# A folded Fourier transform: matmuls of 32 rows in four tiles in place of 64 rows in two

## The chip, the cores and the metric

The kernel runs on one core of a Trainium2 chip. The core has a matrix engine (PE; its weight loads are shown apart as PEld), three engines for elementwise work (VectorE, shown as DVE; ScalarE, ACT; GpSimd, POOL) and SyncE (SP), which here only issues DMAs. Matmuls write to PSUM, eight banks of 2 KB per partition; all other on-chip data lie in SBUF. [...] The metric is the device time of one execution in microseconds; lower is better. All data are float32.

## The reference

```python
batch, seq, dim = (8, 3008, 256)
X = np.fft.fft(x, axis=1)
X = np.fft.fft(X, axis=2)
x = X.real.reshape(8 * 3008, 256)
gate = 1.0 / (1.0 + np.exp(-(x @ w_gate)))      # w_gate, w_val: 256 x 1536
val = x @ w_val
out = gate * val @ w_out                        # w_out: 1536 x 256
```

A real Fourier transform over 3008 positions and over 256 features, and behind it a gated feed-forward layer.

## The kernel before

**Transform.** M = 1504 is half the sequence. By the symmetries of cosine and sine, positions and features are folded: rows that share a table entry up to sign are added first (`fold_ops`, line 398, mostly on POOL), and a matmul then contracts fewer rows against a table of cosines and sines. Batch 0 contracts 128 partitions x NQ = 6 row groups. Batches 1 to 7 are folded once more: `mirror_x` (line 151) writes a copy of x to DRAM, `XR`, in which partitions 0 to 63 hold even rows, 64 to 127 odd ones, and row groups 3 to 5 the mirrored rows; `load_x` (line 144) brings it back as tile `x4`. `turn` (line 449) adds to the odd block a multiple of the even one with VectorE (L454).

The matmuls of one batch are `whole` (line 531), called for the odd and the even block (`blk` 1, 0) and for cosine and sine (`what` 0, 1). `both` (line 493) issues 12 matmuls of about 63 rows x 189 columns each time: the even rows into bank `ev`, the odd rows into bank `od`, on the two halves of the array. The bank pair changes with `what`. `then` (line 507) copies with ACT (L512, L518), adds with VectorE (L514) and `places` (line 522) writes the outputs to rows of `pk` and `qk` (L524, L528), which hold the transform of one batch with 1505 frequencies.

**Feed-forward.** The work behind it goes in *fronts*. A front i is one block of 128 of the 1536 hidden features for one chunk of up to 252 frequencies; 12 fronts make a chunk and 6 chunks, 72 fronts, a batch. In the code and in the prediction a front of a batch is counted from the batch's first front, `s0`. Each front does, in this order of recording:

- `front_a` (line 631): PE, four records `pf<-pk` into one of three `pf` banks, after `seed` (line 622, L629) on ACT has written a starting value there.
- `gate_a` (line 651) of the front before: ACT sigmoid L658, DVE subtraction L659.
- `part` (line 640): ACT copies `pf` to `ae` (L644). Then the seed of the next front.
- `gate_b` (line 666) of the front before: DVE product L671, ACT sigmoid L672, DVE product L675, then sums on POOL (L681).
- `back` (line 714): PE, ten records `po<-h` or `po<-sf` of the output matmul, five fronts late. After the last group of a chunk the five `po` banks are copied out by ACT and DVE (L748).
- `front_b` (line 646): PE, four records `pf<-qk` into the same bank, after `part`.
- two or three jobs from the list `later`: the sums of `finish` on DVE (L765), transposes (L773), and stores.
- the side jobs that `at(i, ...)` has put on this front.

So the order on each engine is written out by hand: an engine takes its instructions in the order in which they are recorded, and waits on semaphores inside it. The side jobs fix where the next batch's fold, its turn, its transform and its loads stand. The transform of batch b + 1 is put at front g0 = s0 + 40 of batch b (at 64 for b = 0), after `front_b`. The matmul of the transform uses the same `po` banks as `back`, which is why it stands where a chunk has just been finished. Tables for batches 1 to 7 are loaded and built during batch 0 (`table_again`, line 193, and `table_odd`, line 206).

## Time and profile before

| | |
|---|---|
| median of 3 runs | 1923.05 us (1923.03 to 1923.23) |
| span of the profiled execution | 1921.4 us |
| DVE, ACT, POOL busy | 74%, 70%, 79% |
| PE records of the transform, batches 1 to 7 | 672 `ev` and `od` matmul records in all |
| DVE additions L514 in it | 56, 17.1 us |
| DVE L454 (`turn`) | 42, 29.1 us |
| DVE sums L765 | 920, 430.5 us, 500 ns each |
| POOL sums L681 | 2392, 1334 us |
| DMA | 97.02 MB, mean 50 GB/s |
| PE clock granted | 1.00 |

A row of a timeline reads: start, duration, engine, line, operation, output<-inputs, shape and number; in brackets idle time before it and what ended it. The trace shows two records for each matmul. Most matmuls are recorded on line 134, in the helper `mm`, so they are told apart by the names of their tiles. The duration of a record contains latency: back to back, a record takes the distance between two starts. The profiled span lacks what lies around it: the median of the runs is 1.65 us longer.

### The profile page before, as it was taken

Reading aid. Unit: us, or ns where it says so; the run is one execution under the profiler, and the core shown is the slowest. Engines: PE = TensorE matmul, PEld = TensorE weight load, DVE = VectorE, ACT = ScalarE, POOL = GpSimd, SP = SyncE. Lnnn points to the kernel's source line nnn. Section 1 sums busy time; section 2 is a strip of 40 time slices with the busy share of each in tenths; the row PEclk is TensorE's granted clock in tenths of the full one; section 3 lists DMA queues with packets and bytes.
Section 4 is the critical chain, followed back from the end, with each engine's and each line's share of the span. In section 5 each row is a group of like instructions: output and inputs, shape, how many; then the busy total and the mean of one; then the engine's idle time right before and its main releaser. Section 6 shows DMA issues by size and latency. Waiting matters only on the chain.

```text
span 1921.4 us, 34211 instructions
## 1 busy us (share of the span) xinstructions
PE 1910.5 (99%) x11164; PEld 1776.2 (92%) x11164; DVE 1429.4 (74%) x3225; ACT 1344.2 (70%) x3148; POOL 1524.8 (79%) x2733
## 2 busy tenths in 40 slices
PE   8999999999999999999999999999999999999999
PEld 5789999999999999999999999999999999999998
DVE  7677877787777777778677777777777687777775
ACT  4876767767777677776777767777677767777775
POOL 2489969978898788987888878888788977877770
PEclk9999999999999999999999999999999999999999
DMA  8353222120131211202111121121200100011011
GB/s 313 110 98 78 66 80 60 48 80 15 22 78 23 80 20 41 61 14 82 26 47 48 20 84 19 47 52 23 80 15 15 27 15 15 14 21 21 15 16 31
DMA packets 173633, 97.02 MB, mean 50 GB/s; under 512 B 134429, under 2 KB 164360, under 8 KB 171664
## 3 DMA queue, kind: packets, MB, share of 16 engines
q1 hardware_dynamic: 172878, 94.32, 20.2%
q8 instruction: 90, 1.47, 0.3%
q14 instruction: 87, 0.71, 0.1%
q10 hardware_dynamic: 546, 0.51, 0.1%
q0 software_dynamic: 32, 0.00, 0.0%
HBM read 70.08 MB, written 46.71 MB: 61 GB/s over the span
## 4 chain that ended last, share of the span: by engine, by line
PE 98%; DMA 1%; DVE 1%; ACT 0%; issue 0%; SPq 0%; ACTq 0%
PE pf L134 51%; PE po L134 43%; PE ev L134 3%; DMA x<-in_xf_dram 1%; PE od L134 1%; PE ps L134 1%; DMA raw<-in_moe_w_val_dram 0%; PE pe L134 0%; DVE z L659 0%; DVE wf L307 0%; ACT wl L389 0%; DVE x L418 0%; DVE x L469 0%; DVE x L405 0%; ACT ae L644 0%
## 5 line engine op out<-in xcount | busy, mean ns | idle before, releaser
L681 POOL TENSOR_TENSOR sf<-h 128x168 f32<-128x168 f32 (+1 forms) x920 | 511.0, 575 | 215.5 <-DVE h L675 215.2
L681 POOL TENSOR_TENSOR sf<-h,sf 128x168 f32<-128x168 f32 (+1 forms) x1104 | 616.4, 579 | 56.5 <-DVE h L675 56.2
L134 PE MATMUL pf<-pk,G 128*128 128x252 f32 (+1 forms) x2304 | 582.7, 376 | 0.0
L134 PE MATMUL pf<-qk,G 128*128 128x252 f32 (+1 forms) x2304 | 582.1, 375 | 0.2 <-ACT ae L644 0.2
L675 DVE TENSOR_TENSOR h<-pf,z 128x252 f32<-128x252 f32 (+1 forms) x576 | 241.7, 420 | 418.5 <-ACT pf L672 418.5
L629 ACT ACTIVATE pf<-ek,ge 128x252 f32<-128x252 f32 (+1 forms) x1142 | 538.1, 471 | 20.4 <-DMA ge<-G 1.0
L134 PE MATMUL po<-sf,wf 128*128 128x168 f32 (+1 forms) x2944 | 508.2, 305 | 0.0
L644 ACT ACTIVATE ae<-pf 128x504 f32<-128x504 f32 (+1 forms) x576 | 339.7, 590 | 233.8 <-PE pf L134 232.5
L134 PEld LDWEIGHTS pf<-pk,G 128*128 128x128 f32 x2304 | 436.7, 190 | 52.6 <-issue 2.3
L134 PEld LDWEIGHTS po<-sf,wf 128*128 128x128 f32 x2944 | 453.4, 190 | 8.0
L134 PE MATMUL po<-h,wf 128*128 128x168 f32 (+2 forms) x2584 | 459.6, 306 | 0.0
L134 PEld LDWEIGHTS pf<-qk,G 128*128 128x128 f32 x2304 | 411.0, 190 | 30.4 <-issue 1.8
L765 DVE TENSOR_TENSOR c<-c 128x168 f32<-128x168 f32 (+1 forms) x920 | 430.5, 500 | 4.8
L134 PEld LDWEIGHTS po<-h,wf 128*128 128x128 f32 x2584 | 411.4, 190 | 17.0 <-issue 0.9
L659 DVE TENSOR_TENSOR z<-ae,pf 128x504 f32<-128x504 f32 (+1 forms) x576 | 383.7, 666 | 33.2 <-ACT h L658 31.7
L658 ACT ACTIVATE h<-pf 128x252 f32<-128x252 f32 (+1 forms) x576 | 218.2, 379 | 163.5 <-PE pf L134 159.4
L672 ACT ACTIVATE pf<-z 128x252 f32<-128x252 f32 (+1 forms) x576 | 214.2, 372 | 79.5 <-DVE h L671 76.6
L671 DVE TENSOR_TENSOR h<-h,pf 128x252 f32<-128x252 f32 (+1 forms) x576 | 233.0, 404 | 0.0
L681 POOL TENSOR_TENSOR sf<-sf 128x168 f32<-128x168 f32 (+1 forms) x184 | 106.0, 576 | 14.4
L681 POOL TENSOR_TENSOR sf<-sf,h 128x168 f32<-128x168 f32 (+1 forms) x184 | 100.7, 547 | 0.0
L748 ACT COPY c<-po 128x504 f32<-128x504 f32 (+1 forms) x138 | 78.5, 569 | 0.0
L773 DVE STREAM_TRANSPOSE os<-c 128x256 f32<-128x256 f32 x188 | 72.4, 422 | 0.4 <-issue 0.3
(139 smaller groups left out, 899.8 us busy)
## 6 DMA issues: line engine op xcount, KB each, us to landing
x<-xr SPq DMA_DIRECT2D x14, 1536.0 KB
out_dram<-os SPq DMA_DIRECT2D x368, 56.0 KB
xr<-in_xf_dram SPq DMA_DIRECT2D x14, 768.0 KB
xr<-in_xf_dram SPq DMA_DIRECT2D x35, 256.0 KB
ek<-ed SPq DMA_DIRECT2D x40, 126.0 KB
out_dram<-os SPq DMA_DIRECT2D x284, 7.0 KB
x<-in_xf_dram SPq DMA_DIRECT2D x3, 1024.0 KB
st<-in_stab_dram SPq DMA_DIRECT2D x3, 753.0 KB
```

Source lines behind the costliest of these rows:

```text
L134: nc.tensor.matmul(o, l, r, start=start, stop=stop, skip_group_check=True)
L629: nc.scalar.activation(PF[i][:, g], EK[i // NFT], AF.Copy, scale=ge[:, g, f : f + 1])
L644: nc.scalar.activation(AP[i], PF[i], AF.Copy, scale=2.0)
L658: nc.scalar.activation(H[p][:, fh, 0:n], PF[i][:, 0], AF.Sigmoid)
L659: nc.vector.tensor_tensor(z[:, :, ::-1], AP.pop(i), PF[i], op=ALU.subtract)
L671: nc.vector.tensor_tensor(h[:, fh, 0:n], h[:, fh, 0:n], pf[:, 1], op=ALU.mult)
L672: nc.scalar.activation(pf[:, 0], z[:, 0], AF.Sigmoid)
L675: nc.vector.tensor_tensor(h[:, fh, n:], pf[:, 0], z[:, 1], op=ALU.mult)
L681: nc.gpsimd.tensor_tensor(block(p, dst), block(p, a), block(p, b), op=(ALU.subtract, ALU.add)[op])
L748: (nc.vector.tensor_copy if t == 1 or t == 3 else nc.scalar.copy)(C[0][:, 3 * t * R : 3 * (t + 1) * R], PO[t][:, 0 : 3 * R])
L765: nc.vector.tensor_tensor(t[:, dst * R : (dst + 1) * R], *v, op=(ALU.subtract, ALU.add)[op])
L773: nc.vector.transpose(os_[0][:, s, 0:nb, h, :], t[:, c0 : c0 + nb * TB])
```

## The change

Batches 1 to 7 are folded once more, row s with row 376 - s. A batch's rows then lie in four groups of 32 partitions (even and odd rows, each plain and mirrored at 376), and each matmul contracts 31 or 32 rows against about 95 table columns, one group into one PSUM bank. What the fold would have to add across partitions before the matmuls is added in part before (`more`) and in part after them.

- `mirror_x` issues 23 DMAs per batch and not 9, of 32 rows each and not 64.
- `table_rows` writes mirrored table rows to DRAM in batch 0; `table_again` loads the tables in 16 DMAs and not 4, and `table_ops` builds them on DVE, POOL and ACT in fronts 45 to 52.
- `swap`: 16 DMAs per batch exchange halves of `x4` between partition groups. `more`: 15 `scalar_tensor_tensor` instructions per batch on DVE add a multiple of what was exchanged: nine of 256 columns, six of 128. `turn` stays and comes earlier.
- `whole` now issues all 96 matmuls of a batch at one place, in four stages of 24. The four tiles take turns from instruction to instruction. After each stage two banks are copied to SBUF by ACT and two by DVE.
- `whole_ops` adds the parts later, from SBUF: 28 instructions on DVE per batch, at fronts s0 + 48 to s0 + 51 and s0 + 60 to s0 + 63 (for batch 1 at 66 to 69 and 72 to 75, half of them on POOL).
- The transform stands after `front_a` of front g0 + 1, and the `back` of front g0 is recorded ahead of `gate_b`.

```diff
+            def swap(blk):
+                hs, here, there = (((1, 3), slice(0, HD), slice(HD, D)), ((0, 2), slice(HD, D), slice(0, HD)))[blk]
+                for g, par, lo in TILES:
+                    o = lo + (TB, -TB)[g]
+                    for h in hs:
+                        nc.sync.dma_start(out=x4[lo : lo + TB, h, :, there], in_=x4[o : o + TB, h, :, here])
+
+            def more(v, blk, c, q):
+                here, there = ((slice(0, HD), slice(HD, D)), (slice(HD, D), slice(0, HD)))[blk]
+                here, there = (v[..., ds] for ds in (here, there))
+                nc.vector.scalar_tensor_tensor(out=here, in0=there, scalar=c[:, q : q + 1], in1=here,
+                                               op0=ALU.mult, op1=ALU.add)
...
-    def whole(b, blk, what):
-        _, then, both = seq_group(b, blk, what, (2, 3) if what else (0, 1))
-        both()
-        return then()
+    def whole(b):
+        ps = [bank("sum", t + 1) for t in range(4)]
+        n = 4 * NQ4
+        for blk in (1, 0):
+            for what in range(2):
+                for part in range(2):
+                    for q in range(N3):
+                        for t, (g, par, lo) in enumerate(TILES):
+                            rows = slice(lo, lo + TB - ((par, q) in ((0, 2), (1, 1), (1, 2))))
...
+                            c0 = (2 * what + 1 - part) * NQ4
+                            mm(ps[t][:, c0 : c0 + tab.shape[-1]], W[b, blk][what][rows, w], tab,
+                               what == part == q == 0, q == N3 - 1)
+                for t, (g, *_) in enumerate(TILES):
+                    cs = slice(2 * what * NQ4, 2 * (what + 1) * NQ4 - (not blk and (g + what) % 2))
+                    (nc.scalar.copy, nc.vector.tensor_copy)[t // 2](TAB["sums"][:, blk, t, cs], ps[t][:, cs])
...
+            t0, swaps, last = (47, (54, 57), 59) if b == 0 else (s0 + 24, (s0 + 29, s0 + 30), s0 + 35)
             for i, f in enumerate(TURN.pop(b + 1)):
-                at(58 + i if b == 0 else slots[-1] - 1 + i * 4 // 6, f)
+                at(t0 + i if b == 0 else t0 + i * 4 // 6, f)
+            swaps_, more = MORE.pop(b + 1)
+            for i, f in zip(swaps, swaps_):
+                at(i, f)
+            for i, f in enumerate(more):
+                at(last + i * 5 // 6, f)
...
-        for blk in (1, 0):
-            at(g0, *[lambda b=b, blk=blk, what=what: whole(b + 1, blk, what)() for what in range(2)])
+        mid[g0 + 1] = lambda b=b: whole(b + 1)
+
+        def ends_(b=b, g0=g0):
+            low, high = whole_ops(b + 1, (nc.vector, nc.gpsimd) if b == 0 else (nc.vector, nc.vector))
+            n0 = g0 + (2 if b == 0 else 8)
+            for i, f in enumerate(low):
+                at(n0 + i, f)
+            n0 = g0 + (8 if b == 0 else 20)
+            for i, f in enumerate(high):
+                at(n0 + i, f)
...
+        if i + 1 in mid:
+            back((i - 5) // 3, (i - 5) % 3)
         if i:
             gate_b(i - 1, *join.pop(i, []))
         for f in pre.pop(i, []) + out_use.pop(i, []):
             f()
-        if i >= 5:
+        mid.get(i, lambda: None)()
+        if i >= 5 and i + 1 not in mid:
             back((i - 5) // 3, (i - 5) % 3)
```

## The prediction

> **What bounds the kernel now.** I read the first part of the page, then the waits, then the timeline of single engines around one transform and around one place where PE does stall. Part 1 and the chain of waits put the end on PE:

> ```profile
> PE 1910.5 (99%) x11164; PEld 1776.2 (92%) x11164; DVE 1429.4 (74%) x3225; ACT 1344.2 (70%) x3148; POOL 1524.8 (79%) x2733
> ```

> So every microsecond that PE stops issuing is added to the end, and every one that a matmul group loses is gained. The profiled span is 1921.4 us; the runs' median is 1923.05, so 1.65 us lie outside the span, and I add them at the end.

> The timeline of PE, batch 1:

> ```profile
> 256.78 0.42 PE L134 MATMUL ev<-st,x 63*128 63x189 f32 x1
> 256.79 0.42 PE L134 MATMUL od<-st,x 63*128 63x189 f32 x1
> 257.04 0.32 PE L134 MATMUL ev<-st,x 63*128 63x189 f32 x1
> 257.05 0.32 PE L134 MATMUL od<-st,x 63*128 63x189 f32 x1
> ...
> 265.05 1.10 PE L134 MATMUL pf<-pk,G 128*128 128x246 f32 x4
> ```

> A matmul leaves two records. The two members of a pair start 0.01 us apart, pairs follow each other every 0.16 us (257.04, 257.20, ...): 48 pairs, 8.27 us from 256.78 to 265.05. That is what the change can shorten, seven times 8.27 = 57.9 us.

> DVE works in a fixed round per front i: subtraction L659, product L671, wait for ACT's sigmoid, product L675. Where DVE is late the round has no slack left. From the timelines of DVE and then ACT, at fronts 40 to 45 of batch 0:

> ```profile
> 196.61 0.88 DVE L528 TENSOR_TENSOR er<-a 7x376 f32<-7x376 f32 x1
> 197.42 0.66 DVE L659 TENSOR_TENSOR z<-ae,pf 128x504 f32<-128x504 f32 x1
> 198.01 0.40 DVE L671 TENSOR_TENSOR h<-h,pf 128x252 f32<-128x252 f32 x1
> 198.86 0.42 DVE L675 TENSOR_TENSOR h<-pf,z 128x252 f32<-128x252 f32 x1 [0.45 <-ACT pf L672]
> 199.20 0.57 DVE L765 TENSOR_TENSOR c<-c 128x168 f32<-128x168 f32 x2
> ```
> ```profile
> 198.44 0.39 ACT L672 ACTIVATE pf<-z 128x252 f32<-128x252 f32 x1 [1.39 <-DVE h L671]
> 198.76 0.36 ACT L658 ACTIVATE h<-pf 128x252 f32<-128x252 f32 x1
> 199.02 0.58 ACT L644 ACTIVATE ae<-pf 128x504 f32<-128x504 f32 x1
> ```

> The reader is to see two numbers. The round takes 199.20 - 197.42 = 1.78 us at its shortest. And ACT's copy L644 of two fronts later stands behind that sigmoid in ACT's order: it ends at 199.60, and PE, which needs it for `front_b`, starts at 199.66 instead of 199.48. So with X(i) the time at which PE has issued `front_b(i)` (194.03 here) and e(i) the end of DVE's round after X(i), PE is stopped by about e(i) - 5.0 us (here 199.20 - 194.03 = 5.17, stop 0.18). A front of 252 columns takes 3.13 us (1565.30 to 1568.43), so besides the round DVE has 3.13 - 1.78 = 1.35 us per front for other work, and a reserve of 5.0 minus its usual e of 3.23 (1562.28 - 1559.05).

> **The change, part by part.**

> *Matmuls.* 96 of 32 rows x 95 columns replace 48 of 63 x 189 per batch: 192 records in 48 quads. Pairs are at the pace of their columns (2 x 189 in 160 ns), so a quad is estimated at 160 x 95/189 = 80 ns, 3.85 us for all, if four run at once as two do. No row shows four. Bounds: 80 ns, and 160 ns if starting four records takes twice a pair's time. I take 80, as pair members start 0.01 us apart. Alone this would save about 4.3 us a batch, 30 us.

> *The wait that it adds.* All four stages of 24 matmuls write the same four PSUM banks, and in the program as built each bank's first matmul of a stage waits for the copy out of that bank after the stage before: tiles 0 and 1 for ACT, 2 and 3 for DVE. (Today two pairs of banks take turns.) A stage is 12 quads, 0.95 us; its end lies some 0.2 us after the last issue, then two copies per engine of 190 columns: 0.32 us, started 0.21 apart (ACT L512), about 0.30 and 0.26 apart on DVE (between L514's 188 columns in 0.345 and L748's 504 in 0.671), plus 0.05 for the signal. From one stage to the next 0.95 + 0.2 + 0.56 + 0.05 = 1.75 us. The first copies are worse: in both engines' orders they stand behind the round of front 40. What waits behind PE's first held matmul is all of PE, `back`, `front_b(41)` and on.

> If DVE came on time (e = 3.23), the whole would start at T0 = X(40) + 0.94 (`front_a(41)` and the switch), DVE would be free at T0 + 2.3, stage 2 would start at 2.3 + 0.6 = 2.9, the end would be 2.9 + 2 x 1.75 + 0.95 = 7.35: 0.9 us better than 8.27, not 4.3.

> *The 15 additions from swapped rows (`more`)*, on DVE in fronts 35 to 39: nine of 256 columns, six of 128. L454 (same operation, 256) takes 0.57 us from start to start as the mean of the six around 239 to 254 (0.37 to 0.69; 0.69 over all 42); for 128 I take 0.40 (bounds 0.22 and 0.45). Other work there: two sums L765 0.90 (mean 0.468 by busy time), two transposes 0.70, copy L748 0.59. Beside the round:
> front 35: 0.70 + 0.45 + 4 x 0.57 = 3.43, so e = 3.23 + 3.43 + 1.78 - 3.13 = 5.31;
> 36: 0.90 + 1.14 = 2.04, e 6.0; 37: 0.70 + 1.37 = 2.07, e 6.7; 38: 1.42, e 6.8; 39: 0.59 + 1.37, e 7.4; 40: 0.59 + 0.90, e 7.5.
> PE is stopped 6.8 - 5.0 = 1.8 us before the transform, T0 is X(40) + 2.74, DVE is free at T0 + 4.8, stage 2 starts at T0 + 5.4, the end is 5.4 + 3.5 + 0.95 = 9.85. Together 1.8 + 9.85 - 8.27 = **+3.4 us a batch, +23.8 for seven**. Bounds: with undisturbed operations (0.37, 0.22, sums 0.28) no stop before T0 and the end at T0 + 7.9, -0.4; with 0.69, +5.

> *What takes the place of L514 and `places`.* Today DVE does these beside PE's matmuls (259.36 to 266.4). Now they read SBUF and stand in fronts 48 to 51 and 60 to 63: in the first group fourteen additions of 188, two of 376, four of 95. The nearest row, L765 (both inputs in SBUF, 168), takes 0.28 alone (271.46: two in 0.57) and 0.54 while POOL folds (535 to 548), and POOL folds the next batch in exactly these fronts. With 0.30/0.47/0.20 for the three sizes e reaches 5.4, a stop of 0.4 us; with 0.56/0.73/0.46, e = 5.9, 8.2, 9.5, 11.3, 11.6, a stop of 6.6. I take 0.40/0.60/0.26: PE's stops also starve POOL of sums, so its share falls. Then e = 4.8, 6.4, 6.75, 7.7, 7.7: **+2.7 us, in six batches +16.2**. Group two (two of 376, four of 95, two of 188) fits: e stays below 5.

> A row first: sums on DVE take 0.28 us while POOL idles, 0.5 while it runs. [...]

> *Moved at no cost.* Mirror copies: 23 DMAs of half the rows instead of 9 on SP; they end fronts ahead of the load, as now. `swap`: 16 DMAs on SP issued at fronts 29 and 30, used at 35 and 37, 15 us later; SP's issue of one takes 0.3 to 0.65 us. Table loads: 16 instead of 4 from 181.5 on (4 took 2.61 us of SP), needed by DVE at front 45, about 197; DVE's wait for four small copies at front 47 and POOL's table work in fronts 45 to 52 (about 10 us over a slack of 0.6 a front) are once only: 0, upper bound +8. Batch 1's first additions on POOL at fronts 66 and 67: POOL's sums are ready some 6 us before PE takes them (516.94 against 523.2), so they fit.

> **Sum.** 23.8 + 16.2 + 0 = +40.0; 1921.4 + 40.0 + 1.65 = **1963 us**.

> **Rivals.**
> 1. *Faster: DVE absorbs the additions* and e stays 3.23 in front 40. Then 7 x -0.9 = -6.3: **1917**. For it: DVE is idle 418.5 us before L675. Against: most of that, 0.45 x 576 = 259 us, is the round's own wait. It decides if an addition of 256 costs below about 0.37.
> 2. *Cancelling:* undisturbed prices, -0.4 x 7 + 0.4 x 6 = 0: **1923**.
> 3. *Four records cannot start in 80 ns.* At 160, stages 2 to 4 grow by 0.97 each, 2.9 us a batch, on top of my sum: **1983**. Against: 0.01 us between pair members. [...]
> 4. *The change does not do what it says:* the four tiles run one after another, 320 ns a quad, stages 2 to 4 each 2.9 us longer, 61 in all: **2024**. Against: pairs do overlap.

> **Chances.** Forecast 0.58, rival 1 0.23, rival 2 0.07, rival 3 0.08, rival 4 0.04. Measured against no change, which this kernel's runs can tell from about 0.2% (3.8 us): faster 0.23, same 0.07, slower 0.70. The range goes from rival 1 with a little more, 1915, to the upper prices of `more` (+35) and of the first group (+40), 1998.

> **What would show it.** Right: PE idle before matmuls of `sum` with releasers ACT and DVE copies, the first of them above 2 us; PE stops on L644's successor at fronts 37 to 40 and 49 to 53 of each batch; the first stage's 12 quads in about 1 us. Wrong: additions at 0.37 and no stop at fronts 48 to 53 (rival 1 or 2); quads at 160 ns (3); a stop on a DMA or a table operation of many us in batch 0, which I priced at nothing.

## The result, and the profile after

The changed kernel takes **2080.85 us** (median of 4 runs, 2077.45 to 2083.22) against 1923.05: ratio 1.0819, 95% interval 1.0803 to 1.0834. The direction was forecast, the size was not: +158 us measured, +40 expected. The profiled run has a span of 2075.7 us, 154.3 above that of before.

Parts 1 and 2 of the page after (row `PEclk`: one digit per slice of 52 us, 9 is full speed), and below them the clock row of the page before:

```profile
PE 1987.4 (96%) x11836; PEld 1818.6 (88%) x11836; DVE 1583.2 (76%) x3475; ACT 1332.6 (64%) x3166; POOL 1565.2 (75%) x2763
PEclk9999889999999899998999989999999998999999
PEclk9999999999999999999999999999999999999999
```

PE is still the bound, but no longer 99% busy, and its clock is no longer full throughout. The clock row is what I had not read as something that a change can move. The timeline of PE around the transform of batch 3 and the windows around it (width, then busy time and records of PE, PEld, DVE, ACT, POOL, then the granted clock, DMA share and GB/s) show why:

```profile
711.12 2.11 PE L134 MATMUL sum<-st,x 32*128 32x95 f32 x48
715.29 10.31 PE L134 MATMUL sum<-st,x 32*128 32x95 f32 x144 [2.07 <-ACT st L630]
725.53 3.17 PE L134 MATMUL po<-h,wf 128*128 128x168 f32 x10
728.49 1.55 PE L134 MATMUL pf<-qk,G 128*128 128x252 f32 x4
```
```profile
709.09:712.50 3.41, 3.35 (x43) 2.51 (x44) 2.96 (x7) 1.96 (x6) 2.76 (x5) 1.00 0.02 5
712.50:715.91 3.41, 1.34 (x29) 1.18 (x24) 2.93 (x8) 2.29 (x7) 1.52 (x3) 1.00 0.00 0
715.91:719.33 3.42, 3.42 (x49) 3.18 (x50) 0.74 (x3) 0.54 (x2) 2.15 (x5) 0.50 0.00 0
...
726.15:729.57 3.42, 3.42 (x13) 3.25 (x12) 0.66 (x3) 0.00 (x0) 0.00 (x0) 0.50 0.85 284
729.57:732.98 3.41, 3.41 (x20) 3.21 (x20) 1.26 (x3) 2.11 (x5) 0.00 (x0) 1.00 1.03 440
```

Stage one runs, PE waits 2.07 us for ACT's copy, and in the next window of 3.41 us the granted clock is 0.50 (two windows like it stand at the dots). It stays there until the tiles are done and for one window of the feed-forward after them (ten `po` records in 2.96 us from start to start, where 1.43 is usual). All clock changes of the trace lie on a grid of 3.413 us. In the kernel after 133.1 us run at half clock, in the one before none until the last matmul. The records of the four tiles (a quad) start within some 20 ns, 7 ns apart; from one quad to the next it takes 112 ns at full clock and 213 ns at half clock.

The other place, fronts 50 to 52 of batch 2, first PE, then DVE:

```profile
757.86 1.12 PE L134 MATMUL pf<-qk,G 128*128 128x252 f32 x4 [0.55 <-ACT ae L782]
...
764.74 2.05 PE L134 MATMUL pf<-qk,G 128*128 128x252 f32 x4 [3.46 <-ACT ae L782]
766.58 1.89 PE L134 MATMUL pf<-pk,G 128*128 128x252 f32 x4
```
```profile
752.30 2.72 DVE L640 TENSOR_TENSOR st<-st 128x188 f32<-128x188 f32 x4
755.05 0.65 DVE L602 TENSOR_TENSOR pk<-st 128x376 f32<-128x376 f32 x1
...
758.08 3.42 DVE L640 TENSOR_TENSOR st<-st 128x188 f32<-128x188 f32 x4
761.54 0.55 DVE L602 TENSOR_TENSOR qk<-st 128x376 f32<-128x376 f32 x1
```

Each burst of additions takes 3.4 to 4.0 us of DVE's order, ACT's copy L782 comes late, PE stops for 0.55 and 3.46 us, and the matmuls behind the stop are again at half pace (2.05 us where 1.12 stood a front earlier).

The same fronts of batch 1 show that this half pace costs nothing here:

```profile
506.02 1.12 PE L134 MATMUL pf<-qk,G 128*128 128x252 f32 x4 [0.55 <-ACT ae L782]
...
512.91 1.12 PE L134 MATMUL pf<-qk,G 128*128 128x252 f32 x4 [3.48 <-ACT ae L782]
...
516.93 1.12 PE L134 MATMUL pf<-qk,G 128*128 128x252 f32 x4 [0.60 <-ACT ae L782]
...
521.93 1.12 PE L134 MATMUL pf<-qk,G 128*128 128x252 f32 x4 [1.58 <-ACT ae L782]
```

The clock stays at 1.00 behind a stop of 3.48 us, and PE then stops twice more, because DVE is late for the whole stretch. Fronts 50 to 56 lose 7.38 us in batch 1, with no half clock, and 7.40 us in batch 2, with 6.83 us of it: PE at half pace only waits less. In the transform, where PE itself is the bound, it does cost: five of the seven, with four windows of half clock each, lose 8.15 to 8.33 us against the kernel before, the two with three windows 6.64 and 6.65. A window of half clock thus costs 1.6 us there, half its length, and the 26 windows together about 42 us, an estimate.

**Where the 154 us lie.** The first matmul of `front_a` starts 576 times in each trace. I took each step from front to front in the kernel after minus the same step in the kernel before and summed by place:

| place | forecast | measured |
|---|---|---|
| fronts 37 to 39 ahead of each of seven transforms (61 to 63 for batch 1) | 7 x 1.8 = 12.6 | 16.6 |
| transform itself, fronts 40 to 42 | 7 x (9.85 - 8.27) = 11.1 | 54.5 |
| fronts 50 to 56 of batches 1 to 6 | 16.2 | 43.0 |
| batch 0, fronts 44 to 60 (tables) | 0, at most 8 | 20.3 |
| all others (fronts 57 to 71 7.5, 67 to 71 of batch 0 4.8, first 37 of batch 1 5.9) | 0 | 19.5 |
| sum (the prediction has 40.0 before rounding by row) | 39.9 | 153.9 |

### The profile page after: what moved, and what is told of

It reads as the page before. It is cut to its first block, busy times and chain, and to the rows that moved or that the text cites. A ratio compares the mean times of both kernels' runs of the same rounds, so it can differ in the third digit from the quotient of the medians.

```text
span 2075.7 us, 36139 instructions
## 1 busy us (share of the span) xinstructions
PE 1987.4 (96%) x11836; PEld 1818.6 (88%) x11836; DVE 1583.2 (76%) x3475; ACT 1332.6 (64%) x3166; POOL 1565.2 (75%) x2763
## 4 chain that ended last, share of the span: by engine, by line
PE 67%; DVE 21%; ACT 5%; DMA 3%; issue 1%; SPq 1%; POOL 1%; DVEq 0%; ACTq 0%; POOLq 0%
PE pf L134 34%; PE po L134 28%; DVE c L903 4%; DVE z L797 4%; PE sum L134 3%; ACT pf L810 3%; DVE x L536 3%; DVE h L813 2%; DVE st L640 2%; DVE h L809 2%; DVE qk L640 1%; DVE c L886 1%; DMA rtab<-in_stab_dram 1%; ACT pf L767 1%; DVE os L911 1%
## 5 line engine op out<-in xcount | busy, mean ns | idle before, releaser
L819 POOL TENSOR_TENSOR sf<-h,sf 128x168 f32<-128x168 f32 (+1 forms) x1104 | 625.7, 586 | 172.2 <-DVE h L813 170.6
L819 POOL TENSOR_TENSOR sf<-h 128x168 f32<-128x168 f32 (+1 forms) x920 | 518.4, 582 | 210.6 <-DVE h L813 210.3
L134 PE MATMUL pf<-qk,G 128*128 128x252 f32 (+1 forms) x2304 | 598.7, 383 | 61.0 <-ACT ae L782 60.3
L134 PE MATMUL pf<-pk,G 128*128 128x252 f32 (+1 forms) x2304 | 590.1, 379 | 0.0
L134 PE MATMUL po<-sf,wf 128*128 128x168 f32 (+1 forms) x2944 | 514.5, 308 | 0.9 <-POOL sf L819 0.8
L134 PEld LDWEIGHTS pf<-qk,G 128*128 128x128 f32 x2304 | 414.1, 192 | 109.6 <-ACT ae L782 77.5
L134 PEld LDWEIGHTS pf<-pk,G 128*128 128x128 f32 x2304 | 435.7, 192 | 60.6 <-ACT pf L767 3.2
L134 PE MATMUL po<-h,wf 128*128 128x168 f32 (+2 forms) x2584 | 471.7, 312 | 0.0
L134 PEld LDWEIGHTS po<-sf,wf 128*128 128x128 f32 x2944 | 459.6, 192 | 10.1 <-POOL sf L819 1.6
L782 ACT ACTIVATE ae<-pf 128x504 f32<-128x504 f32 (+1 forms) x576 | 339.1, 589 | 181.3 <-PE pf L134 179.8
L903 DVE TENSOR_TENSOR c<-c 128x168 f32<-128x168 f32 (+1 forms) x920 | 443.6, 514 | 4.8
L134 PEld LDWEIGHTS po<-h,wf 128*128 128x128 f32 x2584 | 421.7, 195 | 18.3 <-issue 2.1
L819 POOL TENSOR_TENSOR sf<-sf 128x168 f32<-128x168 f32 (+1 forms) x184 | 103.9, 565 | 14.4
L134 PE MATMUL sum<-st,x 31*128 31x95 f32 (+3 forms) x1344 | 84.6, 374 | 14.9 <-ACT st L630 14.4
L134 PEld LDWEIGHTS sum<-st,x 31*128 31x128 f32 (+1 forms) x1344 | 77.3, 278 | 22.8 <-ACT st L630 18.9
```

The costliest lines, as they stand in the source:

```text
L134: nc.tensor.matmul(o, l, r, start=start, stop=stop, skip_group_check=True)
L782: nc.scalar.activation(AP[i], PF[i], AF.Copy, scale=2.0)
L819: nc.gpsimd.tensor_tensor(block(p, dst), block(p, a), block(p, b), op=(ALU.subtract, ALU.add)[op])
L903: nc.vector.tensor_tensor(t[:, dst * R : (dst + 1) * R], *v, op=(ALU.subtract, ALU.add)[op])
```

## The experiments

Three explanations at the start. **C**: a stop of PE lowers the clock, so each stop is paid twice. Rivals: **F**, the 32-row tiles lower the clock by themselves; **S**, the tiles are slow at any clock. "Steps" are those of the table above, in the same order: 16.6, 54.5, 43.0 and 20.3 in the kernel after.

**1. No copies between stages** (`e1_no_stage_wait`).

```diff
-                for t, (g, *_) in enumerate(TILES):
+                for t, (g, *_) in enumerate(TILES) if not blk and what else ():
...
```

> The changed kernel with the copies of the first three stages left out: the four banks are copied once, after the fourth stage, so no matmul of a transform waits for a copy (the sums of the odd block are lost). Theory C (a PE stop that leaves a clock window of 3.41 us less than about 45% busy halves the granted clock in the next one): no stop of 2.07 us, so the granted clock stays 1.00 in the transforms, 48 quads at 112 ns = 5.4 us instead of 14.4, and the first 3.4 us behind it at full pace (1.7 us): about 10.7 us a batch less, 7 x 10.7 = 75, time about 2006. Rival F (the 32-row tiles themselves lower the clock, few rows being busy): the clock falls one window into the tiles, transform about 9 us, tail 1.7: 5 us a batch, about 2046. Rival S (213 ns a quad is the price of the tiles at any clock): 10.3 us, clock 1.00: 4 us a batch, about 2053.

2014.01 us, ratio to before 1.0474 (1.0458 to 1.0490). Steps 16.9, **-9.9**, 42.6, 18.1: only the transform has changed, by 64 us. Its PE timeline and windows:

```profile
937.09 6.78 PE L134 MATMUL sum<-st,x 32*128 32x95 f32 x192
943.80 1.41 PE L134 MATMUL po<-h,wf 128*128 128x168 f32 x8
```
```profile
936.65:940.06 3.41, 3.34 (x95) 2.85 (x93) 2.92 (x7) 2.00 (x5) 2.31 (x5) 1.00 0.02 5
940.06:943.47 3.41, 3.41 (x108) 3.41 (x102) 0.91 (x3) 0.38 (x1) 1.97 (x4) 1.00 0.02 5
```

The same 192 records take 6.7 us from start to start in place of 14.4, at clock 1.00: S falls, and F in its plain form. I had expected 5.4, and 2006 us. Of the 48 quads 36 take 112 ns and 12 take 160 to 171: those are the ones that read every fourth column of the table (`ev`).

**2. Without `more`** (`e3_no_more`; the loop over `more` in `folds` is taken out).

> The changed kernel without the 15 additions `more` of each batch (their part of the sums is left out); the swaps stay. Theory C: the stops of fronts 37 to 39 go (2.3 us a batch), DVE reaches its first copy some 2.5 us earlier, the stop behind stage one is about 1.4 us, its window is above 45% busy and the clock stays 1.00 (another 4.8 + 1.7 + 0.7): about 9.5 us a batch, 7 x 9.5 = 66, about 2015. Rivals F and S, where the clock or the pace does not depend on the stop: 2.3 + 0.7 = 3 us a batch, about 2060.

2035.22 us, 1.0572 (1.0546 to 1.0597), where 2015 was expected. Steps -0.1, **31.0**, 42.6, 20.0. The stops ahead of the transform go, as expected; the clock does not hold, which was not expected. Timeline and windows:

```profile
946.32 1.59 PE L134 MATMUL sum<-st,x 32*128 32x95 f32 x48
948.55 2.31 PE L134 MATMUL sum<-st,x 32*128 32x95 f32 x48 [0.64 <-ACT st L630]
951.05 2.28 PE L134 MATMUL sum<-st,x 32*128 32x95 f32 x48 [0.20 <-ACT st L630]
953.54 3.26 PE L134 MATMUL sum<-st,x 32*128 32x94 f32 x48 [0.20 <-ACT st L630]
```
```profile
946.82:950.23 3.41, 2.77 (x78) 2.61 (x78) 1.96 (x6) 1.86 (x6) 1.96 (x4) 1.00 0.00 0
950.23:953.65 3.42, 3.02 (x67) 2.69 (x64) 1.01 (x4) 1.02 (x4) 1.08 (x3) 1.00 0.02 5
953.65:957.06 3.41, 3.41 (x49) 3.24 (x50) 0.58 (x3) 0.61 (x3) 0.00 (x0) 0.50 0.00 0
```

A window in which PE counts as busy for 3.02 of 3.42 us is followed by half clock, though its stops are 0.20 us each. So C's "45% busy" is not the rule for tiles.

**3. Copies ahead of the round** (`e5_copies_first`).

```diff
+        mid.get(i, lambda: None)()
         if i:
             gate_b(i - 1, *join.pop(i, []))
...
-        mid.get(i, lambda: None)()
```

> The changed kernel with one edit: the transform and its copies are recorded ahead of gate_b of the front before, so that the copies of stage one stand behind one subtraction of DVE and not behind a whole round (nothing is left out). Theory C: the stop behind stage one falls from 2.07 to about 1 us, its window is about 60% busy, the clock holds in the transform: 1 + 4.8 + 1.7 = 7.5 us a batch less, 7 x 7.5 = 52, about 2028, if the delayed round gives nothing back. Rivals F and S: about 1 us a batch, 2074.

2061.77 us, 1.0727 (1.0711 to 1.0744), where 2028 was expected. Steps 16.4, **38.9**, 42.6, 19.1. The stop shrinks by 1 us, and the clock falls all the same in all seven transforms. C as I had it does not hold.

**4. Without the additions** (`e4_no_adds`; `low` and `high` are called for b = 0 alone, and POOL clears `pk` and `qk`).

> The changed kernel without the 28 additions from SBUF in batches 2 to 7 (what they write is zeroed by POOL instead, so those batches are left out); for batch 1 they stay. Theory C: stops and half clock at fronts 50 to 53 and 65 go: 7.5 + 1.1 = 8.6 us in six batches, 51 us, about 2029; of this about 4.5 us a batch is the stop and 3.5 the half clock behind it. Rival (the additions cost only their stops, the clock falls for another reason): 4.5 x 6 = 27, about 2054, and half clock remains at fronts 51 to 54.

2026.50 us, 1.0539 (1.0523 to 1.0554). Steps 16.5, 48.5, **0.0**, 21.3: the 43 us belong to these additions, and with them goes all half clock at fronts 51 to 55 of batches 1 to 6. (The 7.5 us of fronts 57 to 71 fall to 2.5.)

**5. Stops without tiles** (`e2_before_adds`).

```diff
+        for i in range(4 if b else 0):
+            at(g0 + 8 + i, lambda i=i: idle_adds(1, *((188, 188, 188, 188, 376) if i < 2 else (95, 95, 188, 188, 188))))
```

> The kernel before, with 20 extra additions on DVE in fronts 48 to 51 of batches 1 to 6, of the sizes and strides of the changed kernel's first group, on spare SBUF that nobody reads (nothing is left out, and no 32-row tile is in the kernel). If stops of PE alone lower the clock: a stop of about 4 us a batch and half clock for 3.4 to 6.8 us behind it, 7.5 us a batch, 6 x 7.5 = 45, about 1968, with the granted clock at half wherever a window of 3.41 us has less than about 37% of streaming. Rival (the clock falls only in kernels with 32-row tiles): the stops alone, 6 x 4 = 24, about 1947, clock 1.00.

1968.37 us, 1.0236 (1.0221 to 1.0252): +45.7 at fronts 50 to 56 and nothing elsewhere, as forecast. PE and the windows in a kernel that has no 32-row tile:

```profile
700.93 1.65 PE L134 MATMUL pf<-qk,G 128*128 128x252 f32 x4 [3.47 <-ACT ae L653]
```
```profile
697.97:701.38 3.41, 0.45 (x2) 0.43 (x3) 2.89 (x7) 2.12 (x6) 1.23 (x3) 1.00 0.36 58
701.38:704.79 3.41, 3.41 (x11) 2.81 (x10) 2.89 (x7) 1.50 (x5) 2.07 (x6) 0.50 0.00 0
704.79:708.21 3.42, 3.42 (x22) 3.24 (x21) 3.28 (x7) 1.37 (x4) 3.34 (x7) 1.00 0.02 5
```

A stop alone lowered the clock (0.50 behind the 3.47 us), and the additions alone cost what they cost in the kernel after. That the time came out as forecast was luck in one part: I had added a stop of 4 us and 3.5 us of half pace behind it, but five batches lose 7.81 to 7.86 us each, whether 3.41 or 6.83 us of half clock follow. An addition of 188 columns took 0.67 us here (84 in 56.5 us) and 0.71 in the kernel after (76 in 54.0).

**6. Graded stops** (`e6_before_stops`; the same idle additions, other sizes and places).

> The kernel before, with graded DVE bursts on spare SBUF in batches 1 to 6: 5, 6, ... 10 additions of 376 columns in front 27 and 7, 8, ... 12 in front 63 (nothing is left out). At 0.6 us each and 3.1 us of room the stops would be 0 to 2.9 and 1.1 to 4.1 us. The clock should stay at 1.00 behind stops up to about 1.8 us and fall to half for one or two windows of 3.41 us behind those that take more than 63% of one window: some six of the twelve, each for 1.7 to 3.4 us. Sum 24 + 12, about 1959. Rival (a stop below a full window of 3.41 us does not lower the clock): at most two falls, about 1950.

2006.22 us in a single run, where 1959 was expected: an addition of 376 took 0.79 us, not 0.6, so the stops were 2.1 to 7.0 us. The clock held behind the one of 2.13 us and fell behind all eleven from 2.72 us on. A stop of 2.72 us, shorter than one window of 3.41, was enough; the rival falls. It is not the length alone, though: over all runs, four stops of 3.47 or 3.48 us in the feed-forward lowered nothing, the one in batch 1 above among them. Each of them lay across two windows; the one in batch 1 took 0.49 of one and 0.53 of the next.

**7. The gap filled with other matmuls** (`e8_filled`; `whole` is split, `whole(b, 1)` ahead of `gate_b` in front 41, `whole(b, 0)` behind `front_a(42)`).

> The changed kernel with the transform in two parts: the odd block's 48 matmuls in front 41 ahead of gate_b, one copy per bank, then front_b(41) and front_a(42) on PE while the copies run, then the even block's 48, and back(41) behind their copies (nothing is left out). If the stop inside the tiles lowers the clock, and tiles without a stop do not: the clock stays 1.00 in the transforms, which cost 5.4 us of PE in place of 14.4, as in the kernel without stage copies (2014), give or take 1 us a batch where a copy is late: 2010 to 2022. Rival (stopping is not the point, 48 matmuls in one piece cannot hold the clock between other work): clock at half in the transforms, about 2050.

2015.38 us, 1.0482 (1.0466 to 1.0498). Steps 16.4, **-7.2**, 42.5, 22.1, clock 1.00 in all seven transforms: the tiles hold the clock when feed-forward matmuls stand in the gap.

**8. Fewer columns, no stop** (`e10_48_columns`).

```diff
-mm(ps[t][:, c0 : c0 + tab.shape[-1]], W[b, blk][what][rows, w], tab,
+mm(ps[t][:, c0 : c0 + 48], W[b, blk][what][rows, w], tab[..., 0:48],
```

> The changed kernel without the copies between stages, and every transform matmul cut from about 95 columns to 48 (half of the sums are left out). If a quad costs its four records and not its columns: 112 ns a quad as with 95 columns, 5.4 us a transform, about 2014. Rival (a quad costs its columns, as my estimate of 80 ns had it): 57 ns, 2.6 us a batch less, about 1996.

2027.24 us in a single run (half of the sums are left out). The quads take 112 ns with 48 columns as with 95, so the columns are not the price, and my estimate of 80 ns fails. A price per record is not shown either, as the four start 7 ns apart. The traces point to the weight loads: in the kernel before, PEld has

```profile
256.78 0.18 PEld L134 LDWEIGHTS ev<-st,x 63*128 63x128 f32 x1 [0.32 <-issue]
...
256.89 0.19 PEld L134 LDWEIGHTS ev<-st,x 63*128 63x128 f32 x1
```

These two start 0.11 us apart. In the traces of the kernels before and after and of experiments 1, 2 and 8 no weight load of 128 columns starts less than 108 ns after the one before it on the same rows of the array, and every record of a tile has such a load. No run here changes the width of the loads, so this stays an argument. And the time is above experiment 1's, because the clock falls in every transform although PE does not stop:

```profile
1186.38 6.52 PE L134 MATMUL sum<-st,x 32*128 32x48 f32 x192
```
```profile
1188.47:1191.88 3.41, 3.41 (x132) 3.41 (x128) 1.79 (x4) 1.12 (x3) 1.95 (x5) 1.00 0.02 5
1191.88:1195.30 3.42, 3.42 (x29) 3.33 (x26) 1.15 (x5) 0.30 (x2) 1.44 (x3) 0.50 0.43 97
```

So F is half right: what goes with the fall in these runs is not whether PE waits, but how much of a window streams (by the estimate below).

**What rule fits all runs.** Four `pf` records of 252 columns follow each other in 0.85 us, 0.85 ns a column of a record (1.68 us at half clock, behind 766.58 in the kernel after). I let every matmul record stream its columns at that pace (twice as long at half clock), count it by its share of 128 rows, the most that a record of the traces has (a 32-row tile a quarter, the 63 rows of the kernel before a half), and sum for each window of 3.413 us. This is an estimate, but it orders the 13 profiled kernels with changes (7,566 windows, from 20 us on) without one exception, whether a window holds tiles, other matmuls or both. At full clock, 122 windows with a share up to 0.379 are followed by half clock, 7,188 from 0.385 up are not. At half clock, 122 windows from 0.78 up bring the clock back, 134 up to 0.77 do not. In the kernel after alone the edges are 0.378 and 0.385 for the fall, 0.736 and 0.786 for the return; in the kernel before no window is below 0.83. A quad of 95 columns streams 81 of its 112 ns, 0.72; one that reads every fourth column 81 of 169, 0.48; one of 48 columns 41 of 112, 0.36, below the edge without any stop. Windows with tiles in experiments 1 and 7 stay at 0.56 and more; in 2 and 3 one window of each transform falls to 0.36 or less, and the clock with it.

**9. Tables behind the store** (`e9_tables_after_store`).

```diff
-    at(3 * i0 + 6, table_again)
     at(3 * i0 + 8, lambda: later_e[2]())
+    at(3 * i0 + 8, table_again)
...
```

> The changed kernel with one group of edits in batch 0: the 16 table loads are issued on SP two fronts later, behind the store of the row `er`, and the table operations, the turn and the swaps of batch 1 follow 2 to 8 fronts later (nothing is left out). If the stops at fronts 47 to 53 of batch 0 (20.5 us) come from SP's queue (DVE's wait for the loads, and its transpose L911 waiting for the store of `er` that stands behind the 16 loads): two of the three stops go, about 14 us, 2067. Rival (the table operations on DVE and POOL are the cost wherever they stand): 2078 or more.

2069.65 us, 1.0760 (1.0744 to 1.0776). Steps 15.1, 58.1, 42.7, **11.0**: two of three stops go, 9.3 us and not the 14 expected. The table operations, the turn and the swaps were moved in the same edit (not shown), so the run does not part the loads' place from theirs; the traces do. What was removed, in the timelines of DVE and SP of the kernel after, and what stayed, in ACT's chain:

```profile
204.78 0.34 DVE L250 COPY st<-st 128x3 f32<-128x3 f32 x1 [2.93 <-DMA st<-rtab]
...
213.51 0.45 DVE L911 STREAM_TRANSPOSE os<-c 128x256 f32<-128x256 f32 x1 [2.73 <-DMA ed<-er]
```
```profile
188.62 1.19 SPq L233 DMA_DIRECT2D st<-in_stab_dram  x1
...
200.56 0.30 SPq L234 DMA_DIRECT2D st<-rtab  x1
...
206.78 1.08 SPq L728 DMA_DIRECT2D ed<-er  x1
```
```profile
236.42 0.68 ACT L292 ACTIVATE st<-st 128x570 f32<-128x570 f32 x1 [6.80 <-POOL st L287]
```

SP issues the 16 loads from 188.62 to 200.9, then six mirror copies, then the store of `er` at 206.78; the transpose L911 waits for that store. Two of three stops of batch 0 come from SP's queue, the third from the table work on POOL, for which ACT's `halves` waits in the middle of its round; that one is still there, at front 59 (7.4 us more than before).

**10. Everything spread** (`v1_all`, then `v2_pool` and `v3_mixed`). In the first the additions are spread over DVE and POOL one by one; in `v2_pool` all of them stand on POOL from batch 2 on; in `v3_mixed` 16 of the 28 are back on DVE. In the first, as in experiment 7, the load of the next batch stands ahead of the second half, whose rows it can overwrite; the other two put it behind.

> The kernel with the filled transform, and besides: table operations 3 to 9 fronts later, `more` one by one over fronts 32 to 40, the additions from SBUF one by one over fronts 44 to 65, those of the odd block on POOL (nothing is left out). If every stop was a burst in one engine's order: from 2014, 17 us of batch 0 and about 40 of fronts 50 to 53 and 10 of fronts 37 to 39 and 65 go: about 1947, and 1910 if nothing is late any more. Rival (DVE has no room for these additions wherever they stand: round 3.13 - 1.78 = 1.35 us a front, 72 fronts, against about 99 us of work): stops of about 0.5 us spread over many fronts instead, clock 1.00, about 1965.

1973.58 us, 1.0264 (1.0247 to 1.0281).

> The filled transform with the load of the next batch one front later, behind the even block's matmuls; tables as in the kernel with the loads behind the store; `more` one by one; in batches 2 to 7 all 28 additions from SBUF on POOL, one or two a front, outside the fronts in which it folds (nothing is left out). If DVE's lack of room is what is left (3.2 us a batch in the kernel with the additions on DVE) and POOL has it: about 0 a batch, batch 0 about 8, batch 1 about 8 in place of 20 and 14: 1923 + 16 + 1 = 1940. Rival (POOL then delivers its sums late and PE waits for them): 1960 or more. A time below 1923 would need the saving of the transform, 1.8 us a batch, to survive everything else.

1957.24 us, 1.0182 (1.0165 to 1.0199).

> As the kernel with all additions on POOL, but those of the even block (16 of 28) on DVE, at other fronts than in the first such kernel, the late ones two fronts apart. If DVE lacks room: about 2 us a batch more than with POOL, 1952. Rival (it was only the place of the late ones, fronts 57 to 61): the same 1940.

1968.80 us, 1.0239 (1.0224 to 1.0254). All three lie above their forecasts (1947, 1940, 1952). With the additions on POOL the steps are 8.0, **-8.7**, 0.8, 12.2: 10.2 us of half clock are left, and a batch from 2 on costs 0.2 to 2.0 us more than before. The transform saves 1.2 us a batch, `more` takes 1.1 back, and batches 0 and 1 keep 26.5 us. With 16 of the additions on DVE, fronts 50 to 71 cost 13.8 us more, most of it 0.65 to 0.85 us in each of fronts 55 to 57: DVE has no room for them there. No version here beats the kernel before.

## Why the prediction was wrong

- **PE as the bound, a stop counts in full:** right, but PE's time was taken at the full clock throughout, since the row `PEclk` showed nothing else. **This is the step that failed most.** The end of the transform at 9.85 us was summed at full pace; the runs showed 14.4, and half pace in the window behind. Of the 54.5 us at the transforms about 42 are the clock's (26 windows at 1.6 us), and the rest is near the 11.1 forecast. So of the 114 us by which the forecast was short, about 42 are the clock's at the transforms, 27 belong to the first group of additions, 20 to the tables and 20 to places that I had at nothing. PE was busy for 125.8 us under half clock in all, 88.7 of them at the transforms; at the additions it cost nothing, and for the tables no run separates it.
- **Quads at 80 ns:** wrong. 112 ns, and about 169 where every fourth column is read: 6.7 us a transform at full clock, not 3.85. The step was to price a quad by its columns alone and to leave out the weight load that each record brings, 108 ns at the least in the trace that I had. Pair members that start 0.01 us apart said nothing about the rate of a long row of records. The four records of a quad start 7 ns apart, and the quads still follow each other at 112 ns.
- **The stages' wait:** right in kind. Stage two began 4.17 us after the first start (forecast 5.4), held by the copies behind the round of front 40. With 6.7 us of matmuls, 2.07 and two waits of 0.2, a transform at full clock would be about 9.2 us, near the forecast 9.85; two errors cancelled. Measured: 14.4.
- **`more`:** right: 2.4 us a transform against 1.8; 0.60 us for 256 columns (63 in 37.8) against 0.57, 0.54 for 128 (42 in 22.7) against 0.40, above my bound of 0.45.
- **First group of additions:** right place and mechanism, wrong size, the second step that failed: 7.2 us a batch against 2.7, above my upper bound of 6.6. An addition of 188 took 0.71 us where I had taken 0.40 and bounded it at 0.56. The row I started from, L765, writes dense columns; most of these write every second or fourth one, and POOL works beside them. Experiment 6 separates the two for 376 columns that write every second one: a record lasts 0.55 us in 23 cases with POOL at rest, and 0.87 on the mean of 78 in which POOL works for more than half of the time. So most of the price goes with POOL's work.
- **"Once only: 0":** wrong, 20.3 us, above the bound of 8. I counted DVE's and POOL's work but not what stands behind 16 DMAs on SP.
- **"Fits", for the second group and for batch 1's additions on POOL:** not quite. Fronts 57 to 71 lose 7.5 us, and the end of batch 0 and the start of batch 1 10.7. Experiment 4 gives 5.0 of the 7.5 to the additions; the cause of the rest stays open.
- **Rivals:** 1 and 2 fall. Rival 3 held in part (112 to 169 ns, not 160 throughout). 4, tiles in series, looked true by its time and is not: 213 ns a quad is the half clock, and experiment 1 has 112 for the same matmuls.

## What to carry to other kernels

Where PE is the bound, ask of every stop what it leaves of a window of 3.41 us. Where the streaming share of one fell below about 0.38, by the estimate above, the matmuls went at half pace for the next one or two windows in the feed-forward and for three or four in the transforms of the kernel after, and where PE stayed the bound behind the stop, that was paid on top of it, half of each window (1.6 us). Where another engine stayed late anyway, it cost nothing more (7.40 us a batch with it, 7.38 without). Quads of small tiles, at 0.72 or 0.48, sit closer to that edge than full matmuls, at about 1.00, so put full matmuls into their gaps, or leave no gaps. Check a moved DMA against everything that its queue still has to issue, stores included: in experiment 9 the loads behind the store, with the table work moved too, gave back 9.3 us.
